# Clustered attention with a maxout feed-forward: softmax left unnormalised in PSUM, 1/sum spread by TensorE into the value product

## The chip, the cores and the metric

One core of a Trainium2 chip runs the whole program. The metric is device time in microseconds (us) for one execution. The engines are TensorE (PE in the profile, its weight loads PEld), VectorE (DVE), ScalarE (ACT), GpSimd (POOL) and SyncE (SP), which issues the DMAs.

## The reference

Shapes: batch 4, 8 heads, sequence 768, head dimension 64, 16 clusters; the feed-forward has width 512 and hidden width 768.

```python
q_assign = argmax(q_n . c_n); k_assign = argmax(k_n . c_n)       # nearest centroid of each row
scores = scale * q @ k.T
scores = where(q_assign == k_assign, scores, -1e9)
attn = exp(scores - max(scores)); attn = attn / (sum(attn) + 1e-9)
out = attn @ v                                                   # per batch and head
x = out, heads side by side                                      # 3072 x 512
h = maximum(maximum(x @ w1, x @ w2), x @ w3)
return h @ w_out
```

Only keys of the query's own cluster count. The result is float32.

## The kernel before, in words

**Tiles.** A step is one block of 128 queries of one head against all 768 keys: 48 steps per batch, 192 in all. Three blocks of each of two heads make a group of six steps, after which one value product is made (`av`); there are 32 groups. Batch 0 goes through its four head pairs twice, first with query blocks 0 to 2, then with 3 to 5; the other batches take both halves of a pair in turn.

**A step** (`scores`, L472 on). PE writes the scores into a PSUM tile `big` of two banks, three of which rotate: a first product (L478) and a second (L480) that adds the remaining terms and the cluster mask. DVE takes the negated row maximum (L483, `nm`). ACT takes the exponential (L486) from PSUM into an SBUF tile `e`, three of which rotate, with the row sum as a second output `r`. DVE adds 1e-9 and scales (L487), and takes the reciprocal (L488). The normalised row, times 2^14, is then split into two float16 parts in one tile `hl` (three rotate): ACT writes the high part (L496, scaled by `r`) and DVE the low part, `e * r - high` (L497). Some steps, marked `by_pool`, do it otherwise: POOL scales `e` (L492), ACT rounds it (L493) and POOL subtracts (L494). SP issues a DMA that transposes both parts into `pt` (L498), of which three rotate.

**A group's value product** (`av`, L517): 36 matmuls of 384 columns, 18 for each of the two heads, in the two halves of the array's columns, into a PSUM tile `one` of one bank, two of which rotate. ACT evacuates it with the factor 2^-14 (L525, `xs`), and POOL splits it into float16 parts (L527, L528), the input `x16` of the feed-forward.

**The feed-forward** (`ffn_units`): units of 12 matmuls (L552), each in a tile `one`, evacuated by ACT (L562) for w1 and by DVE (L564, a maximum with the one before) for w2 and w3, split by POOL (L570, L571); then 18 matmuls for each block of 128 output rows (L586), evacuated by ACT (L595) and stored.

**Beside it**: each head's inputs are loaded, split and moved (`qk_prep` with L363 and L366, `qk_moves`), the cluster rows found (`cluster_scores`, `cluster_rows`), the values split (`v_prep`, L338 and L339), and in the first batch the weights are loaded and split (L194 to L207). In the first 48 steps four matmuls a step are issued only to keep PE busy (`keep_warm`, L505).

**What sets the order.** All of this is recorded step by step with a priority (`at_prio`); a scheduler then orders each engine's instructions by readiness and priority and waits for free buffers. Each engine runs its own instructions strictly in that order. The numbers that steer it: `AV_LAG` and `AV_LATE` (the value product is recorded two steps after its group), `F_0` and others (over which steps the feed-forward units are spread), and two tables that say which steps go by POOL: `BY_POOL`, one entry for three steps up to step 60 (1: the middle one, 2: the two others), and `MID_POOL`, four entries that repeat after that (3: all three). Before, 12 of the first 27 steps and, after step 60, three of every twelve go by POOL, 45 in all.

Of the kernel before, what the change touches and what calls it, by code (L numbers as in the profile page):

```python
# [23 lines left out]
def kernel(  # L24
# [23 lines left out]
    nc = tc.nc  # L48
# [40 lines left out]
    for c in range(C):  # L89
        nc.gpsimd.memset(rank[:, c : c + 1], float(C - c))  # L90
    onehot = cpool.tile([P, S // 32, 32], F32, name="onehot")
    nc.gpsimd.memset(onehot, 0.0)
# [375 lines left out]

    K2 = D + C

    def scores(b, h, qt, pt, g, by_pool):
        aq, bq, bk, ak = (qkt[b, h // 2][:, j, h & 1] for j in range(4))
        t = big()
        qs = slice(qt * P, (qt + 1) * P)
        for lo, hi in HALF:
            nc.tensor.matmul(t[:, lo:hi], aq[:, qs], ak[:, lo:hi], start=True, stop=False)  # L478
        for lo, hi in HALF:
            last["pe"] = nc.tensor.matmul(t[:, lo:hi], bq[0:K2, qs], bk[0:K2, lo:hi], start=False, stop=True)  # L480
        nm = sb.tile([P, 1], F32, tag="nm", name="nm", bufs=6)
        e = t[:, 0:S]
        last["nm"] = nc.vector.tensor_reduce(nm, e, axis=AX.X, op=ALU.max, negate=True)  # L483
        r = sb.tile([P, 1], F32, tag="r", name="r", bufs=6)
        x = sb.tile([P, S], F32, tag="e", name="e", bufs=3)
        nc.scalar.activation(x, e, AF.Exp, bias=nm, scale=1.0, accum_out=r)  # L486
        nc.vector.tensor_scalar(r, r, 1.0e-9, 2.0**-14, op0=ALU.add, op1=ALU.mult)  # L487
        nc.vector.reciprocal(r, r)  # L488
        pace[:] = [r[0:1]]
        hl = sb.tile([P, 2, S], F16, tag="hl", name="hl", bufs=3)  # L490
        if by_pool:
            nc.gpsimd.tensor_scalar(x, x, r, 1.0, op0=ALU.mult, op1=ALU.mult)  # L492
            nc.scalar.copy(hl[:, 0, :], x)  # L493
            nc.gpsimd.tensor_tensor(hl[:, 1, :], x, hl[:, 0, :], op=ALU.subtract)  # L494
        else:
            nc.scalar.activation(hl[:, 0, :], x, AF.Copy, scale=r)  # L496
            nc.vector.scalar_tensor_tensor(hl[:, 1, :], x, r, hl[:, 0, :], op0=ALU.mult, op1=ALU.subtract)  # L497
        last["dma"] = nc.sync.dma_start_transpose(out=pt[:, g], in_=hl.rearrange("p a s -> p (a s)"))  # L498


    def keep_warm():
# [8 lines left out]
    def av(b, pr, gi, pt):  # L510
# [4 lines left out]
        for n, (kt, va, pa) in enumerate(todo):  # L515
            for i in range(2):
# [6 lines left out]
                )  # L523
        xs = sb.tile([P, NB], F32, tag="xs", name="xs", bufs=1)
        nc.scalar.activation(xs, t[:, 0:NB], AF.Copy, scale=2.0**-14)  # L525
        x = sb.tile([P, 2, NB], F16, tag="x16", name="x16", bufs=9)
# [86 lines left out]
    WO_SPLIT = (0, 0, 0, 1, 1, 0)  # L613
    MID_POOL = (0, 3, 0, 0)
    BY_POOL = (1, 1, 1, 2, 1, 2, 1, 2, 1, 0, 0, 0, 0, 0, 0, 0, 0, 0, 0, 0)

# [9 lines left out]
    P1_LATE, P2_LATE = -10, -10  # L626
    AV_LAG = 2
    PREP, PREP_END, PREP_LATE = 2, 5, -9
    W_LATE, F_LATE, AV_LATE = -5, 0, 2
# [86 lines left out]
    for b, pr, gis in visits:  # L716
        for gi in gis:
            pts = []
            for h in (2 * pr, 2 * pr + 1):
                pt = sb.tile([P, G, 2 * QT, P], F16, tag="pt", name="pt", bufs=3)  # L720
                pts.append(pt)
                for g in range(G):
                    at_prio(step, scores, b, h, gi * G + g, pt, g, by_pool(step))
                    run_step()
                    if step < WARM_END:
                        at_prio(step + 0.6, keep_warm)
                    step += 1
            unit = lambda a=(b, pr, gi, pts): behind("pe", av, *a)
            plan.setdefault(step + AV_LAG - 1, []).append((step + AV_LATE, unit))
# [38 lines left out]
```

## Time and profile before

| | us |
|---|---|
| median of 3 runs | 862.61 |
| lowest and highest run | 861.04, 863.9 |
| profiled execution, first to last instruction (span) | 863.3 |
| PE busy | 742.8 |
| DVE busy | 607.5 |
| ACT busy | 497.3 |
| POOL busy | 484.8 |

The profile gives no time of its own for the profiled execution beside its span; the span lies inside the three runs, so it stands for the whole time.

The page lists busy time and share of each engine, the chain of work that ended last (followed back from the last instruction, at each step to what released it), and groups of equal instructions by source line: busy time, mean duration, and the idle time in front of them with what ended it. Names are `out<-in`. A view by windows gives the busy time of every engine in a stretch, with the clock that PE was granted and the share of time that the 16 DMA engines were busy. A view of waits says who waited for whom, in total, how often, and the longest. PE is busy while a matmul is under way, which is more than the time it costs in a stream: matmuls overlap.

### The profile page before, as it was taken

What the parts mean: (1) busy time and instruction counts of PE and PEld (TensorE: products, weight loads), DVE (VectorE), ACT (ScalarE), POOL (GpSimd) and SP (SyncE); (2) the same over time, 40 slices, a digit from 0 to 9 for tenths busy, and PEclk for the clock granted to TensorE, in tenths of its full rate; (3) what the DMA queues carried; (4) which work ended last, traced back from release to release, by engine and by line L of the source; (5) the groups of instructions that cost most, each with busy time, mean ns of one, the idle gap of its engine ahead of it and who ended that gap; (6) DMA issues with size and microseconds to landing.
All of it is one profiled execution on the core that took longest, in us unless ns stands there. A gap on an engine that the chain in (4) does not pass through costs nothing.

```text
span 863.3 us, 13006 instructions
## 1 busy us (share of the span) xinstructions
PE 742.8 (86%) x4412; PEld 450.9 (52%) x4412; DVE 607.5 (70%) x1135; ACT 497.3 (58%) x827; POOL 484.8 (56%) x470
## 2 busy tenths in 40 slices
PE   3556787897987998888799989898998999999997
PEld 2323454454554655545466556554665566556463
DVE  7889977799898588967788777776786576511020
ACT  6655667775866565757576657575756475510101
POOL 4796672594944466746667556766575555312121
PEclk9966987999999999999999999999999999999999
DMA  6966979999968979897999989689879866900000
GB/s 220 250 143 155 204 143 194 214 256 226 221 127 152 212 129 216 168 188 158 206 162 201 188 204 172 136 171 206 165 148 149 181 110 114 163 36 1 37 1 38
DMA packets 328962, 137.34 MB, mean 159 GB/s; under 512 B 304448, under 2 KB 313664, under 8 KB 328896
## 3 DMA queue, kind: packets, MB, share of 16 engines
q1 hardware_dynamic: 328896, 136.52, 76.3%
q8 instruction: 35, 0.57, 0.3%
q14 instruction: 31, 0.25, 0.1%
HBM read 38.57 MB, written 7.08 MB: 53 GB/s over the span
## 4 chain that ended last, share of the span: by engine, by line
PE 30%; DVE 24%; DMA 18%; POOL 12%; issue 8%; ACT 6%; SPq 2%; POOLq 0%; ACTq 0%; DVEq 0%
PE one L552 13%; DMA pt<-hl 12%; PE one L586 8%; DVE hl L497 6%; DVE nm L483 5%; PE one L517 5%; POOL hl L494 3%; ACT hl L496 2%; ACT e L486 2%; DMA stage<-in_v_dram 2%; DMA wd<-in_moe_w_dram 2%; PE big L478 2%; PE big L480 2%; DVE onehot L439 2%; POOL e L492 2%
## 5 line engine op out<-in xcount | busy, mean ns | idle before, releaser
L497 DVE SCALAR_TENSOR_TENSOR hl<-e,r,hl 128x768 f16<-128x768 f32 x147 | 195.7, 1335 | 67.3 <-ACT hl L496 65.4
L486 ACT ACTIVATE e<-big,nm 128x768 f32<-128x768 f32 x192 | 171.6, 895 | 90.8 <-DVE nm L483 40.6
L552 PE MATMUL one<-x,w16a 128*128 128x384 f16 x1152 | 202.2, 331 | 13.6 <-DVE vf_h L564 8.0
L483 DVE TENSOR_REDUCE nm<-big 128x1 f32<-128x768 f32 x192 | 177.8, 945 | 17.2 <-PE big L480 16.3
L496 ACT ACTIVATE hl<-e,r 128x768 f16<-128x768 f32 x147 | 136.2, 932 | 72.4 <-DMA pt<-hl 54.2
L552 PEld LDWEIGHTS <-w16a 128*128 128x128 f16 x1152 | 110.3, 99 | 95.6 <-issue 28.7
L478 PE MATMUL big<-qk 128*128 128x512 f32 (+1 forms) x384 | 122.0, 399 | 35.6 <-ACT e L486 28.0
L517 PE MATMUL one<-pt,v 128*64 128x384 f16 x1152 | 112.3, 342 | 12.1 <-DMA pt<-hl 5.8
L480 PE MATMUL big<-qk 80*128 80x512 f32 (+1 forms) x384 | 108.1, 361 | 6.6 <-DMA qk<-cl_t 4.3
L552 PE MATMUL one<-x,w16b 128*128 128x384 f16 x576 | 100.7, 329 | 3.9 <-DVE wf_h L564 1.9
L478 PEld LDWEIGHTS big<-qk 128*128 128x128 f32 x384 | 66.0, 200 | 65.8 <-ACT e L486 40.5
L517 PEld LDWEIGHTS <-v 128*64 128x64 f16 x1152 | 71.5, 114 | 52.9 <-issue 20.6
L366 POOL TENSOR_TENSOR qk<-stage,qk 128x768 fp32r<-128x768 f32 x32 | 64.4, 2030 | 47.3 <-ACT qk L363 44.0
L494 POOL TENSOR_TENSOR hl<-e,hl 128x768 f16<-128x768 f32 x45 | 76.3, 1703 | 14.6 <-ACT hl L493 13.2
L552 PEld LDWEIGHTS <-w16b 128*128 128x128 f16 x576 | 55.1, 99 | 44.3 <-issue 11.0
L480 PEld LDWEIGHTS big<-qk 80*128 80x128 f32 x384 | 64.2, 202 | 17.9 <-issue 5.1
L493 ACT CAST hl<-e 128x768 f16<-128x768 f32 x45 | 37.4, 830 | 42.2 <-POOL e L492 34.5
L492 POOL TENSOR_SCALAR e<-e,r 128x768 f32<-128x768 f32 x45 | 44.0, 981 | 31.1 <-DVE r L488 17.9
L564 DVE SCALAR_TENSOR_TENSOR vf_h<-one,vf_h 128x384 f32<-128x384 f32 x48 | 26.4, 550 | 47.6 <-PE one L552 47.5
L505 PE MATMUL one<-ident 128*128 128x512 bf16 x192 | 56.1, 429 | 3.1 <-DVE vf_h L564 2.9
L564 DVE SCALAR_TENSOR_TENSOR wf_h<-one,wf_h 128x384 f32<-128x384 f32 x48 | 26.4, 550 | 43.4 <-PE one L552 43.3
L570 POOL TENSOR_SCALAR wf_h<-wf_h 128x384 f16<-128x384 f32 x24 | 17.1, 714 | 66.3 <-DVE wf_h L564 60.4
(129 smaller groups left out, 967.1 us busy)
## 6 DMA issues: line engine op xcount, KB each, us to landing
stage<-in_qk_dram SPq DMA_DIRECT2D x36, 384.0 KB, 4.2
qk<-qk SPq DMA_DIRECT2D x32, 384.0 KB, 5.6
stage<-in_v_dram SPq DMA_DIRECT2D x25, 384.0 KB, 4.7
wd<-in_moe_w_dram SPq DMA_DIRECT2D x18, 512.0 KB, 4.8
out_dram<-o SPq DMA_DIRECT2D x24, 256.0 KB, 2.6
pt<-hl SPq DMA_TRANSPOSE x192, 4.1
wd<-in_moe_w_out_dram SPq DMA_DIRECT2D x6, 512.0 KB, 4.6
qk<-cl_t SPq DMA_DIRECT2D x56, 48.0 KB, 2.2
```

What stands on the lines that cost most here:

```text
L366: last["lo"] = eng.tensor_tensor(t[:, AQ, i], x, t[:, BQ, i].bitcast(F32), op=ALU.subtract)
L478: nc.tensor.matmul(t[:, lo:hi], aq[:, qs], ak[:, lo:hi], start=True, stop=False)
L480: last["pe"] = nc.tensor.matmul(t[:, lo:hi], bq[0:K2, qs], bk[0:K2, lo:hi], start=False, stop=True)
L483: last["nm"] = nc.vector.tensor_reduce(nm, e, axis=AX.X, op=ALU.max, negate=True)
L486: nc.scalar.activation(x, e, AF.Exp, bias=nm, scale=1.0, accum_out=r)
L492: nc.gpsimd.tensor_scalar(x, x, r, 1.0, op0=ALU.mult, op1=ALU.mult)
L494: nc.gpsimd.tensor_tensor(hl[:, 1, :], x, hl[:, 0, :], op=ALU.subtract)
L496: nc.scalar.activation(hl[:, 0, :], x, AF.Copy, scale=r)
L497: nc.vector.scalar_tensor_tensor(hl[:, 1, :], x, r, hl[:, 0, :], op0=ALU.mult, op1=ALU.subtract)
L517: nc.tensor.matmul(t[D * i : D * i + D, 0:NB], v[:, i, kt, va], pt[i][:, :, pa * QT + kt, :], start=(n == 0), stop=(n == len(todo) - 1),)
L552: nc.tensor.matmul(t[:, 0:NB], w16[jt // JA][:, jt % JA, wa, i, ct], x16[b, gi, ct][:, xa, :], start=(n == 0), stop=(n == 3 * CT - 1),)
L586: nc.tensor.matmul(t[:, 0:DM], h16[jt][:, ha, tt * P : (tt + 1) * P], wo16[0][:, jt, wa, :], start=(n == 0), stop=(n == 3 * JT - 1),)
```

## The change

The exponential is written back into the PSUM tile (`e` is the tile `big` itself), and the split is made from there with the constant 2^14. L487 and L488 of each step are gone. The six row sums of a group are collected in a tile `rs`, and a new function `norm`, recorded one step after the group, turns them into reciprocals (two DVE operations on six columns), splits these into two float16 parts (POOL, two operations), and spreads them with PE: 12 matmuls with a column of `rh`, repeated 64 times, as weights, and a float16 identity as the moving operand, so that every one of 64 rows of a `one` tile holds the reciprocals of 384 queries. ACT copies that to SBUF (`rb`). The value product is evacuated by DVE in place of ACT, multiplied by `rb` on the way. Steps by POOL still use an SBUF tile `e`, of which one is left; their POOL scale uses the constant. `hl` has four buffers in place of three. The tables send nine steps by POOL, all among the first 27, in place of 45.

```diff
+    identh = cpool.tile([P, P], F16, name="identh")
+    nc.gpsimd.tensor_copy(identh, ident)
...
+    PS = 2.0**14
...
-        r = sb.tile([P, 1], F32, tag="r", name="r", bufs=6)
-        x = sb.tile([P, S], F32, tag="e", name="e", bufs=3)
+        r = rs[:, h & 1, g : g + 1]
+        x = sb.tile([P, S], F32, tag="e", name="e", bufs=1) if by_pool else e
         nc.scalar.activation(x, e, AF.Exp, bias=nm, scale=1.0, accum_out=r)
-        nc.vector.tensor_scalar(r, r, 1.0e-9, 2.0**-14, op0=ALU.add, op1=ALU.mult)
-        nc.vector.reciprocal(r, r)
         pace[:] = [r[0:1]]
-        hl = sb.tile([P, 2, S], F16, tag="hl", name="hl", bufs=3)
+        hl = sb.tile([P, 2, S], F16, tag="hl", name="hl", bufs=4)
         if by_pool:
-            nc.gpsimd.tensor_scalar(x, x, r, 1.0, op0=ALU.mult, op1=ALU.mult)
+            nc.gpsimd.tensor_scalar(x, x, PS, 1.0, op0=ALU.mult, op1=ALU.mult)
             nc.scalar.copy(hl[:, 0, :], x)
             nc.gpsimd.tensor_tensor(hl[:, 1, :], x, hl[:, 0, :], op=ALU.subtract)
         else:
-            nc.scalar.activation(hl[:, 0, :], x, AF.Copy, scale=r)
-            nc.vector.scalar_tensor_tensor(hl[:, 1, :], x, r, hl[:, 0, :], op0=ALU.mult, op1=ALU.subtract)
+            nc.scalar.activation(hl[:, 0, :], x, AF.Copy, scale=PS)
+            nc.vector.scalar_tensor_tensor(hl[:, 1, :], x, PS, hl[:, 0, :], op0=ALU.mult, op1=ALU.subtract)
...
+    def norm(b, pr, gi, rs):
+        rr = sb.tile([P, 2 * G], F32, tag="rr", name="rr", bufs=2)
+        nc.vector.tensor_scalar(
+            rr, rs.rearrange("p i g -> p (i g)"), 1.0e-9, 1.0 / PS, op0=ALU.add, op1=ALU.mult
+        )
+        nc.vector.reciprocal(rr, rr)
+        rh = sb.tile([P, 2, 2 * G], F16, tag="rh", name="rh", bufs=2)
+        nc.gpsimd.tensor_copy(rh[:, 0], rr)
+        nc.gpsimd.tensor_tensor(rh[:, 1], rr, rh[:, 0], op=ALU.subtract)
+        t = one()
+        for g in range(G):
+            for a in range(2):
+                for i in range(2):
+                    k = i * G + g
+                    nc.tensor.matmul(
+                        t[D * i : D * i + D, g * P : (g + 1) * P],
+                        rh[:, a, k : k + 1].broadcast_to([P, D]),
+                        identh,
+                        start=(a == 0),
+                        stop=(a == 1),
+                    )
+        rb = rbs[b, pr, gi] = sb.tile([P, NB], F32, tag="rb", name="rb", bufs=2)
+        nc.scalar.copy(rb, t[:, 0:NB])
...
-        xs = sb.tile([P, NB], F32, tag="xs", name="xs", bufs=1)
-        nc.scalar.activation(xs, t[:, 0:NB], AF.Copy, scale=2.0**-14)
+        xs = rbs.pop((b, pr, gi))
+        nc.vector.scalar_tensor_tensor(xs, t[:, 0:NB], PS**-2, xs, op0=ALU.mult, op1=ALU.mult)
...
-    MID_POOL = (0, 3, 0, 0)
-    BY_POOL = (1, 1, 1, 2, 1, 2, 1, 2, 1, 0, 0, 0, 0, 0, 0, 0, 0, 0, 0, 0)
+    MID_POOL = (0, 0, 0, 0)
+    BY_POOL = (1, 1, 1, 1, 1, 1, 1, 1, 1, 0, 0, 0, 0, 0, 0, 0, 0, 0, 0, 0)
...
+    NORM_LATE = 1
...
+            plan.setdefault(step, []).append((step + NORM_LATE, lambda a=(b, pr, gi, rs): norm(*a)))
```

The order of the instructions moves on every engine. Three places show how; line numbers in the changed program are higher by 3 to 35.

DVE in the middle of the program, where three scores of a new group are reduced in one go while feed-forward units (`vf_h`) go on; before (L483 row maximum, L487 and L488 the two operations on `r`, L497 low half):

```order
L483 TENSOR_REDUCE nm<-big 128x1 x3
L487 TENSOR_SCALAR r<-r 128x1
L488 RECIPROCAL r<-r 128x1
L487 TENSOR_SCALAR r<-r 128x1
L488 RECIPROCAL r<-r 128x1
L564 SCALAR_TENSOR_TENSOR vf_h<-one,vf_h 128x384
L487 TENSOR_SCALAR r<-r 128x1
L488 RECIPROCAL r<-r 128x1
L497 SCALAR_TENSOR_TENSOR hl<-e,r,hl 128x768
L483 TENSOR_REDUCE nm<-big 128x1 x2
L497 SCALAR_TENSOR_TENSOR hl<-e,r,hl 128x768
```

The same kind of place now (L486 row maximum, L498 low half, L505 and L508 the reciprocals of a whole group, L551 the value product's evacuation):

```order
L551 SCALAR_TENSOR_TENSOR rb<-one,rb 128x384
L486 TENSOR_REDUCE nm<-big 128x1 x3
L590 SCALAR_TENSOR_TENSOR vf_h<-one,vf_h 128x384
L498 SCALAR_TENSOR_TENSOR hl<-big,hl 128x768
L505 TENSOR_SCALAR rr<-rs 128x6
L508 RECIPROCAL rr<-rr 128x6
L486 TENSOR_REDUCE nm<-big 128x1
L498 SCALAR_TENSOR_TENSOR hl<-big,hl 128x768
L590 SCALAR_TENSOR_TENSOR vf_h<-one,vf_h 128x384
L498 SCALAR_TENSOR_TENSOR hl<-big,hl 128x768
```

The pairs on `r` between maximum and split have gone, one pair per group has come, and the evacuation of the value product is new in this queue.

ACT late in the program, before (L486 exponential, L496 and L493 high half, L525 evacuation of the value product, L562 of a feed-forward unit):

```order
L525 ACTIVATE xs<-one 128x384
L496 ACTIVATE hl<-e,r 128x768
L486 ACTIVATE e,r<-big,nm 128x768
L496 ACTIVATE hl<-e,r 128x768
L486 ACTIVATE e,r<-big,nm 128x768
L496 ACTIVATE hl<-e,r 128x768
L562 ACTIVATE wf_h<-one 128x384
L493 CAST hl<-e 128x768
L486 ACTIVATE e,r<-big,nm 128x768 x3
L493 CAST hl<-e 128x768 x2
```

And now (L489 exponential, into `big`; L497 high half, from `big`; L525 the copy of the spread reciprocals):

```order
L525 COPY rb<-one 128x384
L489 ACTIVATE big,rs<-big,nm 128x768 x2
L497 ACTIVATE hl<-big 128x768
L489 ACTIVATE big,rs<-big,nm 128x768
L497 ACTIVATE hl<-big 128x768
L588 ACTIVATE wf_h<-one 128x384
L497 ACTIVATE hl<-big 128x768
L489 ACTIVATE big,rs<-big,nm 128x768 x2
L497 ACTIVATE hl<-big 128x768
```

The exponentials no longer run three ahead of the high halves; the copy of `rb` stands where the value product's evacuation stood.

PE between the last scores of a group and the value product of the group before, in the dense middle; before (L517 is the value product):

```order
L478 MATMUL big<-qk 128x256
L480 MATMUL big<-qk 128x512
L480 MATMUL big<-qk 128x256
L517 LDWEIGHTS v_3527
L517 MATMUL one<-pt,v_3527 64x384
```

And now (L481 and L483 are the scores, L517 the spread):

```order
L481 MATMUL big<-qk 128x256
L483 MATMUL big<-qk 128x512
L483 MATMUL big<-qk 128x256
L517 LDWEIGHTS rh
L517 MATMUL one<-identh,rh 64x128
```

The load and the matmul of the spread stand 12 times there, and the value product follows them.

More of the change, by code (lines that the diff above doesn't have):

```diff
@@ L469, with scores @@
     K2 = D + C
-    def scores(b, h, qt, pt, g, by_pool):
+    PS = 2.0**14
+    def scores(b, h, qt, pt, g, rs, by_pool):
         aq, bq, bk, ak = (qkt[b, h // 2][:, j, h & 1] for j in range(4))
@@ L495, in scores @@
         else:
-            nc.scalar.activation(hl[:, 0, :], x, AF.Copy, scale=r)
-            nc.vector.scalar_tensor_tensor(hl[:, 1, :], x, r, hl[:, 0, :], op0=ALU.mult, op1=ALU.subtract)
+            nc.scalar.activation(hl[:, 0, :], x, AF.Copy, scale=PS)
+            nc.vector.scalar_tensor_tensor(hl[:, 1, :], x, PS, hl[:, 0, :], op0=ALU.mult, op1=ALU.subtract)
         last["dma"] = nc.sync.dma_start_transpose(out=pt[:, g], in_=hl.rearrange("p a s -> p (a s)"))
+    rbs = {}
+    def norm(b, pr, gi, rs):
[21 more added lines that the diff above has]
+        nc.scalar.copy(rb, t[:, 0:NB])
     def keep_warm():
@@ L718 @@
             pts = []
+            rs = sb.tile([P, 2, G], F32, tag="rs", name="rs", bufs=3)
             for h in (2 * pr, 2 * pr + 1):
@@ L722 @@
                 for g in range(G):
-                    at_prio(step, scores, b, h, gi * G + g, pt, g, by_pool(step))
+                    at_prio(step, scores, b, h, gi * G + g, pt, g, rs, by_pool(step))
                     run_step()
```

## Prediction

> **What bounds the kernel now.** I read the page first: what each engine is busy with, and the chain that ended last.
>
> ```profile
> span 863.3 us, 13006 instructions
> PE 742.8 (86%) x4412; PEld 450.9 (52%) x4412; DVE 607.5 (70%) x1135; ACT 497.3 (58%) x827; POOL 484.8 (56%) x470
> PE 30%; DVE 24%; DMA 18%; POOL 12%; issue 8%; ACT 6%; SPq 2%; POOLq 0%; ACTq 0%; DVEq 0%
> PE one L552 13%; DMA pt<-hl 12%; PE one L586 8%; DVE hl L497 6%; DVE nm L483 5%; PE one L517 5%; POOL hl L494 3%; ACT hl L496 2%; ACT e L486 2%; DMA stage<-in_v_dram 2%; DMA wd<-in_moe_w_dram 2%; PE big L478 2%; PE big L480 2%; DVE onehot L439 2%; POOL e L492 2%
> ```
>
> No engine owns the chain, so an average says little. The busy time by stretch (columns: length, busy time of PE, PEld, DVE, ACT, POOL, granted clock, DMA share, GB/s) says which engine is near full in which stage.
>
> ```profile
> 0.00:250.00 250.00, 181.86 (x902) 106.08 (x903) 214.76 (x388) 162.98 (x267) 172.71 (x184) 0.87 0.89 202
> 250.00:350.00 100.00, 90.90 (x583) 55.64 (x581) 80.67 (x161) 60.27 (x101) 53.28 (x50) 0.98 0.82 166
> 350.00:450.00 100.00, 84.04 (x504) 52.31 (x504) 77.48 (x149) 70.52 (x115) 59.41 (x49) 0.93 0.92 173
> 450.00:750.00 300.00, 278.75 (x1803) 177.71 (x1803) 221.20 (x417) 191.21 (x324) 179.50 (x160) 0.99 0.84 165
> 750.00:863.00 113.00, 107.26 (x624) 59.16 (x622) 13.37 (x24) 12.34 (x22) 19.93 (x29) 1.00 0.11 32
> ```
>
> There are three regimes. Until 250 us DVE is busy 86% beside DMA at 0.89, while PE runs at a mean clock of 0.87: DVE and DMA pace the start. From 450 to 750 us PE is busy 93%. After 750 us there is only the last feed-forward block, PE alone, which the change does not touch. Between 350 and 450 us nobody is full; DMA is nearest.
>
> **The change, part by part.** The prices come from the groups by line (busy us, mean ns of one, idle before).
>
> ```profile
> L497 DVE SCALAR_TENSOR_TENSOR hl<-e,r,hl 128x768 f16<-128x768 f32 x147 | 195.7, 1335 | 67.3 <-ACT hl L496 65.4 <-issue 0.9 <-POOL vf_h L570 0.5
> L483 DVE TENSOR_REDUCE nm<-big 128x1 f32<-128x768 f32 x192 | 177.8, 945 | 17.2 <-PE big L480 16.3
> L564 DVE SCALAR_TENSOR_TENSOR vf_h<-one,vf_h 128x384 f32<-128x384 f32 x48 | 26.4, 550 | 47.6 <-PE one L552 47.5
> L496 ACT ACTIVATE hl<-e,r 128x768 f16<-128x768 f32 x147 | 136.2, 932 | 72.4 <-DMA pt<-hl 54.2 <-DVE r L488 8.3 <-DVE nm L483 4.5
> L493 ACT CAST hl<-e 128x768 f16<-128x768 f32 x45 | 37.4, 830 | 42.2 <-POOL e L492 34.5 <-DMA pt<-hl 6.2 <-POOL hl L494 1.0
> L525 ACT ACTIVATE xs<-one 128x384 f32<-128x384 f32 x32 | 15.5, 483 | 8.9 <-PE one L517 8.9
> L494 POOL TENSOR_TENSOR hl<-e,hl 128x768 f16<-128x768 f32 x45 | 76.3, 1703 | 14.6 <-ACT hl L493 13.2 <-DMA qk<-cl_t 0.9
> L492 POOL TENSOR_SCALAR e<-e,r 128x768 f32<-128x768 f32 x45 | 44.0, 981 | 31.1 <-DVE r L488 17.9 <-DVE r L487 5.5 <-DVE s_w L108 3.6
> ```
>
> *Split from PSUM.* The low half (L497) now takes one operand from PSUM instead of two from SBUF. L564 already has that pattern, on half as many columns: 550 ns. L483 reads 768 columns of PSUM in 945 ns. Both say 0.95 us, against 1.335. The 1.335 is waiting more than work, as the first stretch's DVE groups and one place in the timeline show:
>
> ```profile
> L497 DVE SCALAR_TENSOR_TENSOR hl<-e,r,hl 128x768 f16<-128x768 f32 x39 | 63.8, 1639 | 8.3 <-ACT hl L496 8.2
> L488 DVE RECIPROCAL r<-r 128x1 f32<-128x1 f32 x52 | 7.8, 155 | 0.5
> L487 DVE TENSOR_SCALAR r<-r 128x1 f32<-128x1 f32 x53 | 7.3, 140 | 2.6 <-ACT e L486 2.4
> 55.91 9.36 DVE L497 SCALAR_TENSOR_TENSOR hl<-e,r,hl 128x768 f16<-128x768 f32 x1 [1.00 <-ACT hl L496]
> 56.15 3.53 POOL L339 TENSOR_TENSOR v<-vf,v 128x384 f16<-128x384 f32 x4
> 62.20 2.25 POOL L207 TENSOR_TENSOR w16a<-wf,w16a 128x512 f16<-128x512 f32 x2
> 66.41 0.79 PE L478 MATMUL big<-qk 128*128 128x512 f32 x1 [7.29 <-ACT e L486]
> ```
>
> One split lasted 9.36 us while POOL worked without a break, and PE then stood 7.29 us. L564 runs beside the same POOL and keeps its mean of 550 ns. [...] ACT's high half goes from 932 ns to about 0.81: L525 costs 483 ns for 384 columns and L493 830 for 768. The exponential, 895 ns, now writes to PSUM, which no row shows; a copy's 0.81 us bounds the gain at 0.09 a step, 895 the other end, and I take no gain.
>
> *First 250 us on DVE.* L497: 39 x 0.95 = 37 us instead of 64, so -27. The two small operations per step (L487, L488): -15. Added: three steps fewer by POOL (9 instead of 12), 3 x 0.95 = +3; for each of nine groups an evacuation of 0.55 and two small operations of about 0.15 each, +8. Sum -31 us of 215. DMA, busy 0.89 x 250 = 223 us, allows at most -27 of the span. I take 60% of the DVE sum, **-18** (bounds 0 and -27), since DMA is nearly as full.
>
> *After 250 us on POOL, ACT and DVE.* 33 steps leave POOL for ACT and DVE. DVE stays level: +33 splits at 0.95, but 108 old ones shorter. L494 and L492 hold 5% of the chain, 43 us, about 16 visits at 0.98 + 1.70. 36 of 45 go: -34 us; 13 visits come back as 0.81 + 0.95 = 1.76, +22. So **-12** (0 to -12). A fourth buffer for hl answers part of L496's 54.2 us of waiting for the transposes; I give it nothing of its own.
>
> *The spread of 1/sum on PE.* Per group 12 loads and 12 matmuls of 128 columns. The nearest row is a value product, 36 pairs with 384 columns:
>
> ```profile
> 603.30 3.12 PE L517 MATMUL one<-pt,v 128*64 128x384 f16 x36
> 250.00:350.00 100.00, 3.34 (x24) 0.98 0.82 166
> 450.00:750.00 300.00, 11.82 (x84) 0.99 0.84 165
> ```
>
> The product takes 3.12 us. By columns the spread is 12/36 x 128/384 x 3.12 = 0.35 us, by instructions 1.04; I take 0.7, in between, as neither rate is excluded. The last two rows count L487, one per step, in the two stretches where PE is over 90% busy: 108 steps, 18 groups of six. There it lies on the path: 18 x 0.7 = **+13** (+6 to +19). In the other 14 groups PE's idle time hides it; without that cover it would be 10 more. [...]
>
> Three waits are new. PE's spread waits for POOL's halves of 1/sum, with scores queued behind; ACT's copy `rb` waits for the spread, with exponentials queued behind; DVE's evacuation waits for the value product, with reductions queued behind, where before ACT waited. In the new order each stands one or more scores behind what it waits for, so I add nothing; one hiccup per group of the size that ACT now waits for a product (L525, 8.9 us in 32) would be 0.3 us, 10 us in all.
>
> *The PSUM buffer is held longer.* It was free after the exponential, and is now free after the split.
>
> ```profile
> PE big L478 <- ACT e L486: 12.5, 16, 2.4
> PE one L552 <- DVE vf_h L564: 7.1, 3, 4.5
> PE one L552 <- DVE wf_h L564: 2.6, 4, 1.0
> PE one L586 <- DVE wf_h L564: 1.9, 1, 1.9
> 611.25 0.88 ACT L486 ACTIVATE e<-big,nm 128x768 f32<-128x768 f32 x1
> 614.34 0.93 ACT L496 ACTIVATE hl<-e,r 128x768 f16<-128x768 f32 x1
> 615.35 1.02 DVE L497 SCALAR_TENSOR_TENSOR hl<-e,r,hl 128x768 f16<-128x768 f32 x1 [0.79 <-ACT hl L496]
> 614.34 0.52 PE L478 MATMUL big<-qk 128*128 128x512 f32 x2
> ```
>
> The first four rows are PE's waits from 250 to 750 us. The exponential ends at 612.13, the next score but two starts at 614.34: 2.2 us of slack. The old order's split ends at 616.37, 2.0 us too late; a split right behind the exponential would end at 612.13 + 0.81 + 0.95 = 613.9, just in time. So the cost is 0 if ACT and DVE follow at once, and 2.0 us for a group if not: 23 groups, 46 us, less the 12.5 waited already, +33. Against it stands the 11.6 us that PE waits for L564, which sits behind long splits in DVE's queue. I cancel half of those with a like sum here: **0** (-12 to +33).
>
> **Sum.** 863.3 - 18 - 12 + 13 + 0 = 846 us. The profiled execution's 863.3 lies 0.7 us over the median of the runs, 862.61, and inside them, so no correction is made.
>
> **Rivals.** *PSUM becomes the bound* (slower). One late split in every group after 250 us: 846 + 33 = 879 us. It decides once the time from exponential to end of split passes the 2.2 us of slack. For it: three buffers now cover what three PSUM and three SBUF buffers did, and L496 waits 54.2 us for transposes. Against: r's two operations and POOL's share leave just that link.
>
> *DMA paces the start.* Two stretches of it are full of DMA already:
>
> ```profile
> 150.00:200.00 50.00, 41.21 (x223) 23.96 (x223) 43.80 (x75) 34.76 (x56) 33.48 (x31) 0.93 1.05 232
> 200.00:250.00 50.00, 43.18 (x257) 25.29 (x253) 44.94 (x101) 34.91 (x59) 37.99 (x38) 0.97 0.99 217
> ```
>
> If only the first 150 us gain, -18 becomes -11, and with the spread at its dear end: 863.3 - 11 - 12 + 19 = 859 us. Against: DVE is busy 89% there too.
>
> *Everything is relieved.* Start at -27, POOL -12, spread at its cheap end: 863.3 - 27 - 12 + 6 = 830 us. Against: PE has 21 us idle in 450 to 750 us, so little can be won there.
>
> **How the numbers follow.** Forecast 0.44, PSUM 0.27, DMA 0.15, everything 0.14. The likeliest is 846 us. Low end: 830 less the 11.6 us of L564 waits, 818. High end: the PSUM case's 879. What 0.3% either way (2.6 us, about what a measurement of this kernel tells from no change) makes of the cases: the forecast gives 0.42 faster and 0.02 same, "everything" 0.14 faster, the DMA case 0.06, 0.07 and 0.02 (faster, same, slower), PSUM 0.27 slower. That is 0.62 faster, 0.09 same, 0.29 slower.
>
> **What would show it.** Right: the split's mean near 0.95 us, with no row over 1.1; DVE busy near 184 us until the point where the 54th exponential stands (250 us before), and that point near 232 us; the spread near 0.7 us a group; PE's waits for `big` now ended by the split, under 20 us. Wrong: those waits over 40 us (PSUM), or the start still at 240 us or later with DVE under 80% (DMA). A split that still stretches under POOL would fell the largest term.

## The result and the profile after

The changed kernel takes 874.08 us (median of 4 runs, 867.77 to 879.25) against 863.12 us beside it (4 runs, 861.04 to 863.9): a ratio of 1.0114, 95% interval 1.0069 to 1.0159. It is slower by 1.1%; the forecast was 846 us, faster by 2%. The profile is of the run of 878.35 us, one of the two longer ones.

The page of the changed kernel, the same three lines as before:

```profile
span 876.6 us, 13405 instructions
PE 762.0 (87%) x4796; PEld 462.0 (53%) x4796; DVE 574.5 (66%) x883; ACT 475.0 (54%) x827; POOL 356.6 (41%) x463
PE 43%; DMA 16%; DVE 14%; issue 10%; POOL 9%; ACT 7%; SPq 1%; POOLq 0%; DVEq 0%; ACTq 0%
```

Three engines did lose work, as intended: DVE 33 us, ACT 22, POOL 128. PE gained 19 and its share of the chain went from 30% to 43%. The groups of the changed kernel (busy us, mean ns of one, idle before it):

```profile
L489 ACT ACTIVATE big<-big,nm 128x768 f32<-128x768 f32 x183 | 160.1, 875 | 163.5 <-DVE nm L486 162.0
L498 DVE SCALAR_TENSOR_TENSOR hl<-big,hl 128x768 f16<-128x768 f32 x183 | 172.5, 950 | 62.9 <-ACT hl L497 62.3
L486 DVE TENSOR_REDUCE nm<-big 128x1 f32<-128x768 f32 x192 | 178.4, 949 | 39.5 <-PE big L483 38.1
L497 ACT ACTIVATE hl<-big 128x768 f16<-128x768 f32 x183 | 146.0, 814 | 18.9 <-DMA pt<-hl 16.9
L543 PE MATMUL one<-pt,v 128*64 128x384 f16 x1152 | 113.8, 339 | 19.6 <-DMA pt<-hl 17.5
L517 PE MATMUL one<-identh,rh 128*64 128x128 f16 x384 | 19.4, 233 | 15.9 <-POOL rh L510 12.0 <-ACT wf_h L588 3.2 <-POOL rh L511 0.6
```

PE's matmuls overlap: the 1152 of L543, at 339 ns each, sum to 390 us and keep PE busy for 113.8. Read the rest from the idle columns. Before, ACT's high half waited 54.2 us for transposes and DVE's row maximum 16.3 us for scores. Now ACT's exponential waits 162.0 us for the row maximum, the row maximum 38.1 us for scores, and PE's value product 17.5 us for transposes. The exponential and both halves of the split are shorter and the row maximum is as long as before, but the step is fed later: we read from this that PE has become late with its scores. For comparison, two waits of PE and one group of the kernel before:

```profile
PE big L478 <- ACT e L486: 28.0, 23, 7.3
PE one L517 <- DMA pt<-hl: 5.8, 6, 1.2
L486 ACT ACTIVATE e<-big,nm 128x768 f32<-128x768 f32 x192 | 171.6, 895 | 90.8 <-DVE nm L483 40.6
```

The longest waits of PE over the whole changed program:

```profile
PE big L481 <- DVE hl L498: 23.7, 14, 3.6
PE one L543 <- DMA pt<-hl: 17.5, 8, 4.0
PE one L517 <- POOL rh L510: 12.0, 4, 6.5
```

The stretches of the changed kernel:

```profile
0.00:250.00 250.00, 183.40 (x995) 107.26 (x996) 196.70 (x323) 158.66 (x269) 153.86 (x199) 0.94 0.90 203
250.00:350.00 100.00, 89.20 (x620) 55.88 (x617) 71.84 (x120) 57.66 (x102) 35.81 (x46) 0.98 0.85 168
350.00:450.00 100.00, 87.83 (x558) 54.40 (x559) 68.64 (x100) 58.17 (x101) 32.80 (x43) 0.87 0.85 166
450.00:750.00 300.00, 281.99 (x1901) 176.64 (x1900) 212.60 (x304) 180.26 (x321) 110.87 (x142) 0.98 0.82 160
```

DVE lost 18 us of the first 250 and nothing came of it: counted in the trace, the 54th exponential ends at 250.2 us (249.8 before). Where the time went is seen from the ends of the exponentials in the two traces: the 96th at 407.3 (408.4 before), the 108th at 454.2 (447.9), the 120th at 508.4 (485.9), the last at 766.1 (744.1). The two kernels run level for 400 us, and the exponentials fall 22 us behind in the 24 steps after the 96th, where the third batch starts and the feed-forward of the second begins to stand in PE's queue.

Not all of these 22 us are lost there. In that stretch (101.1 us, 77.5 before) PE is busy 20.3 us longer and idle only 3.3 us longer: it now also does 54 matmuls of the output product, which the kernel before does after its 120th exponential, and 48 of the spread. The blocks of output rows (L595 before, L621 now) are a steadier mark: the 9th is evacuated at 506 us and the 12th at 601 in both kernels, the 15th at 684 before and 693 now, the last at 860 and 872. Over the whole program PE is not even idle longer, 114.6 us now and 120.5 before; it is busy 19.2 us longer, and the spread's rows sum to 19.4. One place in the stretch, in the timeline:

```profile
463.77 0.51 PE L483 MATMUL big<-qk 80*128 80x512 f32 x2
466.06 0.95 DVE L498 SCALAR_TENSOR_TENSOR hl<-big,hl 128x768 f16<-128x768 f32 x1
466.59 0.81 ACT L497 ACTIVATE hl<-big 128x768 f16<-128x768 f32 x1 [2.37 <-DMA pt<-hl]
467.91 3.29 PE L543 MATMUL one<-pt,v 128*64 128x384 f16 x23 [3.63 <-DMA pt<-hl]
469.77 0.96 DVE L498 SCALAR_TENSOR_TENSOR hl<-big,hl 128x768 f16<-128x768 f32 x1 [1.04 <-ACT hl L497]
471.13 0.80 PE L409 MATMUL big<-qk,cw 128*128 128x512 f32 x1
```

PE has written its scores; the next thing in its queue is the value product of a group whose transposes have not landed. It stands 3.63 us, while ACT's high half waits for a transpose too. DVE and ACT finish the scores that are there; when PE goes on, the next free `big` goes to cluster scores (L409), and they get no new ones. The longest stand of the stretch, 6.52 us from 405.1 us, is another: the spread waits for POOL's rounding of the reciprocals, which for 3.6 us of it stands in POOL's queue behind a scaling of the values (L336) that itself waits for its load. And PE is slower behind a stand. After 240 us PE stands six times for over 2.5 us, and each time its granted clock falls to 0.50 within 5 us of the stand's start, for 3.4 to 10.2 us (after the one shown, from 468.7 to 472.1 us: the L409 of the last row takes 0.80 us in it, a like one at 472.15 us takes 0.40). It falls also at 369.7 and 554.1 us, behind stands of 1.82 and 2.41 us.

**How far PE may run ahead** is a figure that the rest of this text uses. Counted in PE's order of instructions, over groups 9 to 31: how many scores are begun between the last score of a group and the last matmul of its value product. Before: 7.4. Changed: 4.3. In the traces, over the middle of the program, a score starts 6.9 us before its exponential in the kernel before and 3.5 us in the changed one, and from the end of a group's last split to the start of its value product it is 9.8 us before and 4.5 us now; a transpose takes 4.2 us from issue to landing (the median in the changed kernel; 4.1 before). The scheduler has three `big`. While the exponential freed them, PE ran seven scores ahead and reached the value product long after its transposes. Since the split frees them, it cannot, and gets there about when they land, eight times before.

### The profile page after: what moved, and what is told of

It is laid out like the page before. It is cut to its first block, busy times and chain, and to the rows that moved or that the text cites. A ratio compares the mean times of both kernels' runs of the same rounds, so it can differ in the third digit from the quotient of the medians.

```text
span 876.6 us, 13405 instructions
## 1 busy us (share of the span) xinstructions
PE 762.0 (87%) x4796; PEld 462.0 (53%) x4796; DVE 574.5 (66%) x883; ACT 475.0 (54%) x827; POOL 356.6 (41%) x463
## 4 chain that ended last, share of the span: by engine, by line
PE 43%; DMA 16%; DVE 14%; issue 10%; POOL 9%; ACT 7%; SPq 1%; POOLq 0%; DVEq 0%; ACTq 0%
PE one L578 18%; PE one L543 8%; PE one L612 7%; DMA pt<-hl 6%; DMA stage<-in_v_dram 6%; DVE nm L486 4%; PE big L481 4%; DMA wd<-in_moe_w_dram 3%; PE big L483 3%; DVE hl L498 3%; POOL qk L368 3%; ACT hl L497 2%; ACT big L489 2%; POOL v L341 1%; PE one L531 1%
## 5 line engine op out<-in xcount | busy, mean ns | idle before, releaser
L489 ACT ACTIVATE big<-big,nm 128x768 f32<-128x768 f32 x183 | 160.1, 875 | 163.5 <-DVE nm L486 162.0
L498 DVE SCALAR_TENSOR_TENSOR hl<-big,hl 128x768 f16<-128x768 f32 x183 | 172.5, 950 | 62.9 <-ACT hl L497 62.3
L578 PE MATMUL one<-x,w16a 128*128 128x384 f16 x1152 | 205.8, 334 | 5.5 <-ACT wf_h L588 2.4
L486 DVE TENSOR_REDUCE nm<-big 128x1 f32<-128x768 f32 x192 | 178.4, 949 | 39.5 <-PE big L483 38.1
L497 ACT ACTIVATE hl<-big 128x768 f16<-128x768 f32 x183 | 146.0, 814 | 18.9 <-DMA pt<-hl 16.9
L481 PE MATMUL big<-qk 128*128 128x512 f32 (+1 forms) x384 | 120.9, 397 | 38.5 <-DVE hl L498 23.7
L543 PE MATMUL one<-pt,v 128*64 128x384 f16 x1152 | 113.8, 339 | 19.6 <-DMA pt<-hl 17.5
L483 PE MATMUL big<-qk 80*128 80x512 f32 (+1 forms) x384 | 107.5, 358 | 1.3 <-DVE qk L452 1.3
L578 PE MATMUL one<-x,w16b 128*128 128x384 f16 x576 | 101.1, 331 | 1.2 <-ACT vf_h L588 0.6
L481 PEld LDWEIGHTS big<-qk 128*128 128x128 f32 x384 | 66.2, 201 | 65.8 <-issue 27.4
L543 PEld LDWEIGHTS <-v 128*64 128x64 f16 x1152 | 68.9, 113 | 56.6 <-issue 18.1
L553 POOL TENSOR_SCALAR x<-rb 128x384 f16<-128x384 f32 x32 | 16.4, 512 | 136.4 <-DVE rb L551 120.8
L368 POOL TENSOR_TENSOR qk<-stage,qk 128x768 fp32r<-128x768 f32 x32 | 58.4, 1842 | 31.1 <-ACT qk L365 26.0
L483 PEld LDWEIGHTS big<-qk 80*128 80x128 f32 x384 | 63.7, 200 | 12.3 <-DVE qk L452 2.0
L378 POOL TENSOR_SCALAR qk<-qk 64x1536 fp32r<-64x1536 f32 x16 | 24.0, 1499 | 70.5 <-PE big L410 22.7
L612 PE MATMUL one<-wo,wf_h 128*128 128x512 f16 x216 | 49.8, 388 | 0.8 <-ACT o L621 0.8
L621 ACT ACTIVATE o<-one,so 128x512 f32<-128x512 f32 x24 | 16.4, 691 | 62.3 <-PE one L612 62.3
```

The source lines that it names most:

```text
L368: last["lo"] = eng.tensor_tensor(t[:, AQ, i], x, t[:, BQ, i].bitcast(F32), op=ALU.subtract)
L497: nc.scalar.activation(hl[:, 0, :], x, AF.Copy, scale=PS)
L498: nc.vector.scalar_tensor_tensor(hl[:, 1, :], x, PS, hl[:, 0, :], op0=ALU.mult, op1=ALU.subtract)
L543: nc.tensor.matmul(t[D * i : D * i + D, 0:NB], v[:, i, kt, va], pt[i][:, :, pa * QT + kt, :], start=(n == 0), stop=(n == len(todo) - 1),)
L578: nc.tensor.matmul(t[:, 0:NB], w16[jt // JA][:, jt % JA, wa, i, ct], x16[b, gi, ct][:, xa, :], start=(n == 0), stop=(n == 3 * CT - 1),)
L612: nc.tensor.matmul(t[:, 0:DM], h16[jt][:, ha, tt * P : (tt + 1) * P], wo16[0][:, jt, wa, :], start=(n == 0), stop=(n == 3 * JT - 1),)
```

## The experiments

Three theories. H: the hold of `big` until the split costs the time, by keeping PE from running ahead. N: the group's norm costs it. T: the two tables cost it. Each edit makes the scheduler lay out the program anew, so that differences of a few us between two kernels are not given a cause here. In all ratios the kernel before, run beside, is 1.

### The parts alone: the split, the tables, the norm

*e1, split from PSUM alone*, in the kernel before:

```diff
-        x = sb.tile([P, S], F32, tag="e", name="e", bufs=3)
+        x = sb.tile([P, S], F32, tag="e", name="e", bufs=3) if by_pool else e
```

> The kernel before with one part of the change: the exponential of the steps that do not go by POOL is written back into `big` and split from there, still scaled by each row's own r (the two small operations stay), with the old tables, old buffers and no norm. Theory H (three PSUM tiles now have to cover everything from the score to the end of the split, so scores cannot run ahead): slower than before, 870 us or more, with PE's waits for `big` ended by the split over 30 us in all. Theory N (the group's norm on PE, POOL, ACT and DVE costs the time): faster than before, about 850 us, since the shorter split stays and the norm is away. Theory T (the tables cost it): also faster, about 850.

Measured: 897.99 us, ratio 1.0403 (1.0359 to 1.0447), +33 us. The waits of PE, and the split:

```profile
PE one L517 <- DMA pt<-hl: 31.9, 15, 3.9
PE big L478 <- ACT e L486: 20.3, 5, 7.3
PE big L478 <- DVE hl L497: 19.1, 13, 5.6
L497 DVE SCALAR_TENSOR_TENSOR hl<-big,r,hl 128x768 f16<-128x768 f32 x147 | 147.2, 1012 | 59.9 <-ACT hl L496 58.5
```

The split got shorter, 1335 to 1012 ns, and DVE 39 us less busy (568.1), and the kernel slower by 33 us. So neither N nor T is needed for a loss. H's time was right and its sign in the profile half right: PE waits 19.1 us for the split, under the 30 expected, and 31.9 us at the value product (L517, 5.8 before), which now stands 4.1 scores behind its group. The hold shows where PE is blocked behind something else. About half of the loss is standing (PE is idle 138.6 us, 120.5 before); the other half is the same 4412 matmuls being busy longer (761.6 us, 742.8 before) at a mean granted clock of 0.937 in place of 0.950.

*e2, the tables alone*, in the kernel before:

```diff
-    MID_POOL = (0, 3, 0, 0)
-    BY_POOL = (1, 1, 1, 2, 1, 2, 1, 2, 1, 0, 0, 0, 0, 0, 0, 0, 0, 0, 0, 0)
+    MID_POOL = (0, 0, 0, 0)
+    BY_POOL = (1, 1, 1, 1, 1, 1, 1, 1, 1, 0, 0, 0, 0, 0, 0, 0, 0, 0, 0, 0)
```

> The kernel before with only the change's two tables: nine steps by POOL in place of 45, everything else as before. Theory T: slower, 873 us or more, as the change. Theories H and N: within 0.6% of before, 858 to 868 us: 36 splits more on DVE at 1.2 to 1.6 us in place of POOL's 2.7 us.

861.78 us, ratio 0.9986 (0.9956 to 1.0015). POOL loses 99 us of work (385.4 left) and nothing changes. T is out on its own, and so is the forecast's gain from POOL.

*e3, the old tables in the changed kernel*, the same lines the other way round:

> The changed kernel with the two tables of before: 45 steps by POOL (each with the one SBUF tile `e`), the rest as changed. Theory T: back at 863 us or less. Theory H: stays slow, 870 us or more; steps by POOL free the PSUM tile at the exponential, but three POOL steps in a row share one `e`, so little is won. Theory N: stays slow, 870 or more.

890.28 us, ratio 1.0311 (1.0259 to 1.0363): 16 us above the change. Harmless in the kernel before (e2), the old tables cost under the hold and the one SBUF `e`; PE waits 22.8 us for exponentials there (9.3 in the changed kernel).

*e4, the changed kernel without norm*:

```diff
-            plan.setdefault(step, []).append((step + NORM_LATE, lambda a=(b, pr, gi, rs): norm(*a)))
...
-        xs = rbs.pop((b, pr, gi))
-        nc.vector.scalar_tensor_tensor(xs, t[:, 0:NB], PS**-2, xs, op0=ALU.mult, op1=ALU.mult)
+        xs = sb.tile([P, NB], F32, tag="rb", name="rb", bufs=2)
+        nc.vector.tensor_scalar(xs, t[:, 0:NB], PS**-2, 1.0, op0=ALU.mult, op1=ALU.mult)
```

> The changed kernel without norm: the row sums are not used, the value product is evacuated by DVE with a constant factor, so the output is not normalised. It takes 384 matmuls of 128 columns, 128 small POOL and DVE operations and 32 ACT copies away. Theory N: 860 us or less. Theory H: the PE time of the spread is won in the full stretches, 18 groups x 0.45 us = 8 us, and no more: 864 to 870 us. Theory T: the same as H.

867.12 us, ratio 1.0042 (1.0016 to 1.0068). All of norm costs 7 us in the changed kernel, where H had 8; without it the kernel is still not faster than before.

*e9, the change without the swap of r for norm* (each step keeps its own `r`), in the kernel before, with e2's lines as well:

```diff
-        x = sb.tile([P, S], F32, tag="e", name="e", bufs=3)
+        x = sb.tile([P, S], F32, tag="e", name="e", bufs=1) if by_pool else e
...
-        hl = sb.tile([P, 2, S], F16, tag="hl", name="hl", bufs=3)
+        hl = sb.tile([P, 2, S], F16, tag="hl", name="hl", bufs=4)
```

> The kernel before with the split from PSUM, the change's two tables, its four hl and its one SBUF `e`, but each step still normalised by its own r and no norm: the change without the swap of r for norm. If the swap is a gain under the hold (r's two operations, 57 us on DVE in all, lengthen the time that `big` is held): 880 us or more, above the change's 874. If the norm is a net cost: 868 us or less.

883.96 us, ratio 1.0226 (1.0179 to 1.0272): the swap gains 10 us under the hold. From e1 and e9 the change can be walked: 863 before, 898 with the hold (e1), 884 with the new tables and the fourth `hl` (e9), 874 with norm in place of r (the change). On this walk the hold is the only step that loses. It is one walk of several, though: the next section but one undoes the hold, and the loss stays.

### The hold without the split from PSUM

*e7 and e8.* Both add to the kernel before one DVE operation of one column behind each low half. In e7, shown here, it reads the PSUM tile (the variable `e` of the code) and so holds `big`; e8 has `x[:, 0:1]` in its place, the SBUF tile that the profile calls `e`.

```diff
             nc.vector.scalar_tensor_tensor(hl[:, 1, :], x, r, hl[:, 0, :], op0=ALU.mult, op1=ALU.subtract)
+            nc.vector.tensor_tensor(nm, e[:, 0:1], hl[:, 1, 0:1], op=ALU.add)
```

> The kernel before, with one added DVE operation of one column behind each low half that does not go by POOL; it reads column 0 of the PSUM tile and of hl (and writes nm, which nobody reads again), so that `big` is held until the split, while the split itself stays in SBUF. Theory H: slower by at least as much as the split from PSUM was (e1, +33 us), since the split here takes 1.3 us in place of 0.95: 895 us or more. If the hold is harmless: as e8.

> The control for e7: the same added operation, but it reads column 0 of the SBUF tile `e`, so `big` is free at the exponential as before. All theories: 147 operations of about 0.15 us on DVE, of which the full stretches pay a part: 862 to 880 us.

e7: 946.25 us, ratio 1.0958 (1.0915 to 1.1002). e8: 886.14 us, 1.0275 (1.0245 to 1.0304). The 60 us between them are the hold, while e7's DVE even worked 47 us less than e8's. Two groups of e7:

```profile
L483 DVE TENSOR_REDUCE nm<-big 128x1 f32<-128x768 f32 x192 | 179.3, 948 | 42.2 <-PE big L480 41.2
L498 DVE TENSOR_TENSOR nm<-big,hl 128x1 f32<-128x1 f32 x147 | 21.3, 149 | 0.9
```

The same two of e8:

```profile
L483 DVE TENSOR_REDUCE nm<-big 128x1 f32<-128x768 f32 x192 | 178.8, 945 | 16.1 <-PE big L480 15.7
L498 DVE TENSOR_TENSOR nm<-e,hl 128x1 f32<-128x1 f32 x147 | 67.8, 466 | 0.5
```

The row maximum waits 41.2 us for scores with the hold, 15.7 without. The value product stands 4.1 scores behind its group in e7, 6.6 in e8. The control was above its expected range, as its small operation cost 67.8 us and not 22; the last section has more on it.

*e6, two `big` in place of three* in the kernel before:

```diff
-    ps_big = ctx.enter_context(tc.tile_pool(name="ps_big", bufs=3, space=PSUM))
+    ps_big = ctx.enter_context(tc.tile_pool(name="ps_big", bufs=2, space=PSUM))
```

> The kernel before with two tiles `big` in place of three and nothing else: the depth alone. Theory H: much slower, since a score cannot run ahead of the exponential any more: 900 us or more, PE's waits for `big` ended by the exponential over 60 us. If depth does not matter: under 875 us.

896.8 us, ratio 1.0408 (1.0368 to 1.0447): H's 900 and its 60 us of waits for exponentials were missed by 3 us each (57.1). One tile fewer costs as much as holding three longer (e1).

### The hold undone inside the change

*e5* lets every exponential go to SBUF again (three `e`; to fit, three `hl` and one `rb`), *e11* does it with two `e` and four `hl`, *e10* is the changed kernel with e5's buffers:

```diff
-        x = sb.tile([P, S], F32, tag="e", name="e", bufs=1) if by_pool else e
+        x = sb.tile([P, S], F32, tag="e", name="e", bufs=3)
...
-        hl = sb.tile([P, 2, S], F16, tag="hl", name="hl", bufs=4)
+        hl = sb.tile([P, 2, S], F16, tag="hl", name="hl", bufs=3)
...
-        rb = rbs[b, pr, gi] = sb.tile([P, NB], F32, tag="rb", name="rb", bufs=2)
+        rb = rbs[b, pr, gi] = sb.tile([P, NB], F32, tag="rb", name="rb", bufs=1)
```

> The changed kernel with the hold undone: every exponential goes to an SBUF tile `e` (three rotate), so `big` is free at its end; norm and the new tables stay, hl goes back to three buffers and rb to one so that it fits. Theory H: the 1.1% come back and more is not sure, since the split then reads two SBUF operands again (1.2 to 1.35 us): 850 to 868 us, PE's waits for `big` ended by the split gone. Theory N: stays at 872 us or more, since the norm is still there.

> The changed kernel with the hold undone at the other price in SBUF: two SBUF tiles `e` for all steps, four hl, one rb. Theory H: 855 to 870 us, under the change. If the split from SBUF (1.15 us in e5 in place of 0.95, 37 us on DVE in all) costs as much as the hold: 874 or more.

> The changed kernel with three hl and one rb, as e5 had: the control for e5. If these buffers made e5 slow: 885 us or more, with ACT's high half waiting over 100 us for transposes. If the split from SBUF made e5 slow: within 0.6% of the change, 869 to 880.

e5: 890.84 us, 1.0314 (1.0281 to 1.0346). e11: 872.57 us, 1.0093 (1.0061 to 1.0125). e10: 890.59 us, 1.0271 (1.0215 to 1.0327). H failed here: with like buffers the undoing brings nothing (e5 as e10; e11, with one `rb` and two `e`, as the change). The fourth `hl` and second `rb` are worth 16 us to the changed kernel. Three groups of e5 show another loop in place of the hold:

```profile
L498 DVE SCALAR_TENSOR_TENSOR hl<-e,hl 128x768 f16<-128x768 f32 x183 | 209.8, 1148 | 75.0 <-ACT hl L497 74.3
L497 ACT ACTIVATE hl<-e 128x768 f16<-128x768 f32 x183 | 153.7, 842 | 133.1 <-DMA pt<-hl 131.7
L486 DVE TENSOR_REDUCE nm<-big 128x1 f32<-128x768 f32 x192 | 177.9, 944 | 13.4 <-PE big L483 12.4
```

The row maximum is fed in time again (12.4 us), but ACT's high half waits 131.7 us for `hl` to be transposed. In e10 the time met the expectation and the wait did not: 38.4 us, read in the longest of its six runs.

*f1 and f2: norm or buffers.* f1 is e5 without norm (the edit of e4, with one `rb`); f2 is e5 with two `rb`, and eight `x16` in place of nine:

```diff
-        x = sb.tile([P, 2, NB], F16, tag="x16", name="x16", bufs=9)
+        x = sb.tile([P, 2, NB], F16, tag="x16", name="x16", bufs=8)
```

> e5 (exponential in SBUF, three `e`, three hl, new tables) without norm, the value product evacuated by DVE with a constant factor: nothing normalises, the output is not normalised. If norm is what made e5 slow (890.8): 855 to 866 us, the level of e2. If the buffers made it slow: 880 us or more.

> e5 with two rb in place of one (eight x16 in place of nine make the room). If the single rb, which binds a group's norm to the value product of the group before, made e5 slow: 860 to 874 us. If it was hl's three buffers: 885 us or more.

f1: 850.63 us, 0.984 (0.9794 to 0.9887). f2: 891.39 us, 1.0273 (1.022 to 1.0326). With the exponential in SBUF it is norm that costs, 40 us, and not the single `rb`; with the hold it cost 7. In PE's order norm moves the value product back from 6.7 scores (f1) to 8.4 (f2); from a group's last split to it are 11.5 us and 17.2. The three `pt` are free only after it.

Put together, hold and norm overlap (us; ratio to the kernel before):

| | without norm | with norm |
|---|---|---|
| exponential to SBUF, no hold | f1: 850.63 (0.984) | e11: 872.57 (1.0093), e5: 890.84 (1.0314) |
| exponential to PSUM, hold | e4: 867.12 (1.0042) | the change: 874.08 (1.0114), e10: 890.59 (1.0271) |

With neither, the other parts win about 14 us. Either one takes that gain away, and the second adds less. So the loss is not the hold's alone: norm without it brings one too (f1 and e5 have the same `e` and `hl`). Across the other cells the buffers differ (three `hl` in f1, e5 and e10, four in e4, e11 and the change; two `e` in e11), so the shares are rough.

*f5: the value product late without norm.* f1 with

```diff
-    AV_LAG = 2
+    AV_LAG = 4
...
-    W_LATE, F_LATE, AV_LATE = -5, 0, 2
+    W_LATE, F_LATE, AV_LATE = -5, 0, 4
```

> f1 (SBUF `e`, three hl, no norm, output not normalised) with the value product recorded two steps later. In PE's order its last matmul then stands 7.9 scores behind its group on average, in place of 6.7 (with norm, in e5 and f2, 8.4). If norm's price there is the late value product, which frees pt late and so holds up the transposes: 870 to 890 us, with ACT's high half waiting over 100 us for transposes. If the place does not matter: 845 to 857, as f1.

858.57 us, 0.9925 (0.9894 to 0.9956): the sign and the wait as expected, the size not. The group of ACT's high half, f1 first:

```profile
L497 ACT ACTIVATE hl<-e 128x768 f16<-128x768 f32 x183 | 152.4, 841 | 96.0 <-DMA pt<-hl 94.5
```

And in f5:

```profile
L497 ACT ACTIVATE hl<-e 128x768 f16<-128x768 f32 x183 | 153.6, 840 | 143.2 <-DMA pt<-hl 142.4
```

The wait grew by 48 us and the time by 8, so the late value product explains about 8 of norm's 40 us. The other 32 stay open.

### DVE, DMA, and the place of the value product

*e12, DVE relieved in the kernel before*:

```diff
-        nc.vector.tensor_scalar(r, r, 1.0e-9, 2.0**-14, op0=ALU.add, op1=ALU.mult)
...
-        nc.scalar.activation(xs, t[:, 0:NB], AF.Copy, scale=2.0**-14)
+        nc.scalar.activation(xs, t[:, 0:NB], AF.Copy, scale=1.0)
```

> The kernel before without the first of r's two operations: the reciprocal alone remains, the factor 2^14 of the split and its inverse at the value product's evacuation are left out, and the 1e-9. It takes 192 operations of 0.14 us from DVE, 27 us. If each us of DVE is paid at the end, as e8 says (147 x 0.15 = 22 us cost 22 us): 836 to 850 us. If only the depth of the buffers counts: 857 to 864 us.

863.69 us, 0.9987 (0.9962 to 1.0012). 27 us less of DVE's work win nothing. The expectation leaned on e8, and e8 does not say it: it added 67.8 us, not 22, and cost 24. In e12's profile, of the longest of its twelve runs (870.28 us), the exponential waits 66.1 us for the row maximum (40.6 before) and the high half 79.3 us for transposes (54.2): what DVE saved seems to have become waiting.

*f3 and f4: half of the transposes' bytes* in the kernel before and in the changed one.

```diff
-        last["dma"] = nc.sync.dma_start_transpose(out=pt[:, g], in_=hl.rearrange("p a s -> p (a s)"))
+        last["dma"] = nc.sync.dma_start_transpose(out=pt[:, g, 0:QT], in_=hl[:, 0, :])
...
-                    pt[i][:, :, pa * QT + kt, :],
+                    pt[i][:, :, kt, :],
```

> The kernel before with only the high half transposed (half the bytes of 192 DMAs); the value product uses the high half in both places, so the output is not exact. If hl's loop (split, transpose, free) and with it the DMA sets the pace of before: 850 us or less, with ACT's high half waiting under 20 us for transposes in place of 54. If PE sets it: within 0.6%, 857 to 868.

> The changed kernel with the same half transpose. If DMA sets its pace as well: it falls as far as f3 or further, 850 us or less. Theory H (PE waits for `big`, which the split frees): little, 864 us or more, since PE's value product waits 17.5 us for transposes in the changed kernel and no more than a part of that is won.

f3: 851.51 us, 0.9855 (0.9822 to 0.9889). f4: 875.15 us, 1.0118 (1.0088 to 1.0148). The kernel before hangs in part on the loop of `hl` (-13 us; the wait of its high half fell to 33.2, not under 20). The changed kernel does not: with a DMA share of 0.52 in place of 0.82 between 450 and 750 us it takes the same time, although the value product's wait for transposes fell from 17.5 to 11.1 us. A shorter wait there is thus not by itself time won; the next run tests the order.

*f6: the value product later in the changed kernel*, by the same two lines as f5.

> The changed kernel with the value product recorded two steps later: its last matmul stands 5.4 scores behind its group in place of 4.3 (7.4 in the kernel before). If the change is slow because PE reaches the value product before its transposes have landed: 860 to 868 us, with PE's waits for transposes under 8 us in place of 17.5. If the hold itself is what costs: within 0.6% of the change, 869 to 880, the waits gone over to scores that wait for the split.

859.22 us, ratio 0.9941 (0.9916 to 0.9967): 15 us under the change and faster than the kernel before. The chain by engine on the page of f6:

```profile
PE 52%; DVE 16%; DMA 14%; ACT 7%; issue 5%; POOL 4%; SPq 2%; POOLq 0%; DVEq 0%; ACTq 0%
```

And its waits of PE over the whole program:

```profile
PE big L481 <- DVE hl L498: 17.7, 9, 5.4
PE one L517 <- POOL rh L510: 13.4, 8, 3.2
...
PE one L543 <- DMA pt<-hl: 5.2, 4, 2.1
```

PE's share of the chain rose from 43% to 52%, and it is idle 100.0 us in place of 114.6. The value product's wait fell from 17.5 to 5.2 us, and the scores' wait for the split fell too, from 23.7 to 17.7, where H wanted it to rise. The hold is still there: a score still starts only 3.4 us before its exponential. From the last split to the value product it is 9.3 us now, nearly the 9.8 of the kernel before, and the 120th exponential ends at 488.9 us (508.4 in the changed kernel). So the place of the value product in PE's queue costs the changed kernel 15 us, more than its whole loss. That the hold put it there is read from the order: 4.1 scores in e1 and e7, 6.6 in the control e8. f5 is the counter-test: the same edit, where PE runs seven scores ahead, makes the kernel slower by 8 us. The kernel before was not run with it.

## Why the prediction was wrong, point by point

- **The split from PSUM, 0.95 us: right.** Its mean is 950 ns and its longest 959 (183 of them), and none stretches beside POOL; L497's longest before was 9358. The high half at about 0.81 (814 ns) and the exponential at no or little gain (875 ns) were right too. With a constant factor the split takes 950 ns from PSUM, and from SBUF (e5) also 949 where no POOL instruction overlaps it (80 of 183); the others bring e5's mean to 1148. So what the split from PSUM saves is time beside POOL: before, the 94 splits that an instruction of POOL overlaps take 1518 ns on average and the 53 others 1010; now the 88 such take 948 and the 95 others 952.
- **First 250 us, -18: failed, 0.** DVE's busy time fell 18 us in it (31 forecast), and the 54th exponential did not move. The step that failed is the inference from "DVE busy 86%" to "DVE paces". e12 says the same with less: of its 27 us about 7 lie in this stage, and its 54th exponential ends at 250.8 us. The DMA rival's sign came (250.2 us, DVE at 79%), but half of the transposes' bytes do not move the stage's end one way: it ends at 256.1 (f3) and 243.4 (f4). In 19 of the 20 kernels of this record it lies between 243 and 262 us, in e7 at 278. What sets it stays open.
- **POOL off the chain, -12: failed, 0** (e2). Work of POOL lay on the chain (12% before), but when it went the chain took another way of the same length (861.78 us).
- **The spread, +13: the sign right, the size half.** 12 matmuls take 0.53 us in the timeline (0.7 forecast), as the row below shows, and norm with its waits costs 7 us under the hold (e4), but 22 to 40 without it (e11 and e5 against f1). "Nothing for the waits" was wrong: PE's spread waits 12.0 us for POOL's halves, 6.5 of them in one place.

```profile
459.71 0.53 PE L517 MATMUL one<-identh,rh 128*64 128x128 f16 x12
```

- **The longer hold, 0: failed, +33 alone in the kernel before** (e1), and this is the step that failed most. The forecast's working took one step at 611 us and its 2.2 us of slack, priced a late split there at 2.0 us for each of 23 groups, and then set the sum to 0 against waits that would go. The rival "PSUM becomes the bound" came near the time with 879 us, and its +33 is e1's figure; both are luck. Its sign in the profile, over 40 us of PE waiting for the split, did not come (23.7 us, 19.1 in e1): PE's order adapts to the hold. The scheduler puts the value product three scores earlier, and moving it back wins 15 us (f6). How much of the changed kernel's time the hold costs beside norm cannot be told exactly, as the two overlap.
- **What the terms add up to.** Where hold and norm are both absent (f1), the rest of the change wins about 14 us, with the split still in SBUF; the forecast had 30 for its two gains.

What was missed is that a buffer's slack at one step says nothing of how far the queue behind it was built to run ahead.

## What to carry to other kernels

A buffer that is held longer takes lead from the engine that fills it (here PE's fell from 7.4 scores to 4.3). Count in that engine's order how far it runs ahead of the point where its own later work needs the results, and ask what will stand there with less lead; then move that work back (f6), or don't hold the buffer. An engine at 86% in a stage is not its pace unless taking its work away moves the stage's end, and one run with such an edit tells it (here DVE lost 18 us of work, and the 54th exponential ended at 250.2 us, 249.8 before).

## What the runs showed that was not expected

**A small DVE operation took five times as long beside POOL as without it** (806 ns and 149 on average in e8). The operation of one column of e8, with two operands in SBUF (count, shortest, median and longest in ns):

```profile
L498 DVE TENSOR_TENSOR nm<-e,hl x147: 110/159/1922, 32.3 to 774.9; 128x1 f32<-128x1 f32 x147
```

The same one in e7, with one of them in PSUM:

```profile
L498 DVE TENSOR_TENSOR nm<-big,hl x147: 113/149/159, 31.0 to 848.6; 128x1 f32<-128x1 f32 x147
```

Sorted by what POOL does in e8's trace, the 71 that overlap with an instruction of POOL (by more than 30 ns) take 806 ns on average and the 76 others 149. In e7 none of the 147 takes over 159 ns. The 9.36-us split of the prediction is one of the 94 that POOL overlaps in the kernel before. What lengthens these operations is not shown. The changed kernel's first operation on a group's sums has one operand, in SBUF, and stretches as well: of its 32, the longest of the 16 that POOL does not overlap takes 174 ns, and this one 3.01 us, while POOL goes from one instruction to the next:

```profile
50.77 3.01 DVE L505 TENSOR_SCALAR rr<-rs 128x6 f32<-128x6 f32 x1 [5.79 <-ACT big L489]
51.95 1.80 POOL L368 TENSOR_TENSOR qk<-stage,qk 128x768 fp32r<-128x768 f32 x1
```

**A constant factor was cheaper than one from a tile of one column**: the low half from PSUM 950 ns against 1012 (the change and e1), the high half from PSUM 814 against 901, from SBUF 842 against 932 (e5 and the kernel before).
